# Left factors on VectorE, decoded weights stored and read back, the split of g on VectorE

## The chip, the cores and the metric

One NeuronCore of a Trainium2 chip. The metric is device time in microseconds of one execution of the whole program, as a median over runs. TensorE (PE in the profile), VectorE (DVE), ScalarE (ACT), GpSimd (POOL) and SyncE (SP) each run their own instructions in order; DMA transfers are issued from the queues of SyncE and ScalarE.

## What is computed

Three stages, all in float32, over 4 batches of 768 tokens (3072 rows):

```python
state = gamma * state + outer(k[t], v[t])      # 8 heads of 64, per head
x[t]  = scale * q[t] @ state                   # -> x, 3072 x 512
h = x @ w_in                                   # 512 -> 2048
y = (h - tanh(h)) @ w_out                      # 2048 -> 512
h2 = y @ w_in2                                 # 512 -> 1024
s = h2 * softmax(h2)
out = ((s - mean(s)) / std(s) * g_ln) @ w_out2 # 1024 -> 512
```

The two 2048-wide products are the first layer, the two 1024-wide ones the second. The weights arrive as 64-bit words; the kernel makes float32 of them itself ("decoding").

## The kernel before

Every float32 operand of a matmul is split into a high part and a low rest (both in the matmul's type), and a product is three matmuls: high by high, high by low, low by high. A split is a cast on ScalarE and a subtraction on another engine (`parts`, lines 158 to 160; for weights `stage3`, 147 to 154). A weight block (128 x 512) is decoded by `stage1` (ScalarE) and `stage2` (four operations of VectorE, lines 136 to 144); class `Decoder` steps through load, stage 1, stage 2, stage 3 for a list of blocks.

The tokens fall into six column blocks of 512 (s = 0 to 5). Blocks 0 and 1 take the plain way: attention and `products_h` (line 342) for all 16 blocks f of w_in, then the loop at line 638, which decodes w_out, splits g (`split_g`: `gh` on ScalarE, `gl` on VectorE) and runs `products_y` (line 369) for both; the results go through `ysb` to `y1d` in DRAM (`keep_y`, ScalarE's queue).

Blocks 2 to 5 take h in pairs by a scheme with seven products for a 2 by 2 block product in place of eight. The left factors are sums of four quarters of w_in. `combine_w` (line 499) makes them for one of 8 pairs j: it loads the decoded blocks j and j + 8 from DRAM (`wfd` to `wq`), forms four sums (`wsum`) on GpSimd, splits everything into `wch` (ScalarE) and `wcl` (GpSimd) and stores the four results to `wcd` in DRAM on SyncE's queue; `load_wl` (line 529) reads them back as `wc`. The blocks of w_in get into `wfd` by line 179, from SyncE's queue. The eight combines run at lines 624 and 649, in the last steps of w_in and during the w_out loop.

The loop at line 730 runs 16 steps (two passes, `q`: block pairs 1 and 2, eight j each). One step is 42 matmuls (`product`), interleaved with the next step's first product, and in pass 1 with attention units (`visit`). A product lands in a PSUM bank; `keep` copies it to `part` on ScalarE before the next product adds to the same bank; `summed` adds on VectorE (`hs`), `finish` (line 703) takes the tanh on ScalarE and subtracts on GpSimd or VectorE, and stores g to `gd` on SyncE's queue. From step 13 on the loop also begins to decode w_out again (`dec1`, line 737).

Then the loop at line 800, 64 steps (s, f), 12 matmuls each: `load_g` reads g from `gd`, `split_p` splits it (`gp`, subtraction on VectorE and GpSimd in turn), `dec1.step()` goes on with decoding w_out, `products_y` adds to four banks. In its later part the second layer's weights are decoded and combined (`com`, `dec2`). Last comes the second layer.

Working tiles come from two pools: `t4`, 40 buffers of 4 KB per partition (raw words, `w`, `wc`, `x`), and `t2`, 15 buffers of 2 KB (`wf`, `gh`, `gl`, `g`, `part`, `hs`, `th`). The order on each engine is set by a scheduler that places the instructions by an estimate of time, except where `pin` keeps program order (the first blocks) and for TensorE's order in the passes, the loop at line 800 and the second layer, which is as written.

```python
    def parts(h, o, src, eng):
        nc.scalar.copy(h, src)
        eng.tensor_tensor(o, src, h.bitcast(F32), ALU.subtract)
```

Of the kernel before, what the change touches and what calls it, by code (L numbers as in the profile page):

```python
# [36 lines left out]
P = 128  # L37
# [53 lines left out]
def body(ctx: ExitStack, tc, z, w_in, w_out, w_in2, w_out2, g_ln, cst, tab, out):  # L91
# [23 lines left out]
    wfd = [yd.tile([P, 2, 512], F32, name=f"wfd{j}") for j in range(NJ1)]  # L115
    wcd = [[yd.tile([P, 4, 256], F32, name=f"wcd{j}_{i}") for i in range(4)] for j in range(NJ1)]
# [45 lines left out]
    class Decoder:  # L162
# [6 lines left out]
        def to(self, st, upto, fixed=False):  # L169
            while self.at[st] < min(upto, self.n):  # L170
# [5 lines left out]
                elif st == 2:  # L176
                    stage2(self.raw.pop(i), self.wf[i], fixed)
                    if self.kept and i < NF1:
                        nc.sync.dma_start(out=wfd[i % NJ1][:, i // NJ1, :], in_=self.wf[i])
                else:  # L180
                    self.w[i] = stage3(self.wf.pop(i), self.scales[i], self.eng, fixed)
# [307 lines left out]
    made = [0]  # L489
# [9 lines left out]
    def combine_w():  # L499

        j = made[0]
        made[0] += 1
# [8 lines left out]
        nc.gpsimd.tensor_tensor(t[:, 0, :], a21, a22, ALU.add)  # L511
        nc.gpsimd.tensor_tensor(t[:, 1, :], t[:, 0, :], a11, ALU.subtract)
        nc.gpsimd.tensor_tensor(t[:, 2, :], a11, a21, ALU.subtract)
        nc.gpsimd.tensor_tensor(t[:, 3, :], a12, t[:, 1, :], ALU.subtract)
        for to, lo, n, src in (
# [6 lines left out]
            parts(h, o, src, nc.gpsimd)  # L522
        for i, u in enumerate(ya + yb):
            n = 3 if i < 2 else 4
            nc.sync.dma_start(out=wcd[j][i][:, :n, :], in_=u[:, :n, :].bitcast(F32))
        if j == 0:
            wl[0] = views(ya, yb)
# [80 lines left out]
    for n in range(NF1):  # L608
# [14 lines left out]
        if n in (NF1 - 4, NF1 - 2, NF1 - 1):  # L623
            combine_w()
# [13 lines left out]
    for n in range(NF1 + 1):  # L638
# [9 lines left out]
        if n in (1, 4, 7, 10, 13):  # L648
            combine_w()
        if n == 6:  # L650
            sums[1] = x_sums(1, nc.gpsimd)
# [51 lines left out]
    def finish(s, f, h, eng):  # L703
# [5 lines left out]
        nc.sync.dma_start(out=gd[s][:, f, :], in_=g)  # L709
# [5 lines left out]

    q = [(p, j) for p in (1, 2) for j in range(NJ1)]
    b1, b2, u2, p1, p5 = {}, {}, {}, {}, {}
    dec1 = Decoder([w_out[f] for f in range(NF1)], [None] * NF1, nc.vector)
# [11 lines left out]
    for n in range(len(q) + 1):  # L730
# [3 lines left out]
        if n + 1 < len(q):  # L734
            load_wl(n + 1)
        if now and p == 2 and j >= 5:
            dec1.step()
# [43 lines left out]
    gs, gp = {}, {}  # L781
    steps = [(s, f) for s in range(2, NSB) for f in range(NF1)]

    def load_g(upto):
        while len(gs) < min(upto, len(steps)):
            s, f = steps[len(gs)]
            t = t2([P, SB], F32, "g")
# [228 lines left out]
```

## Time and profile before

| | us |
|---|---|
| median of 3 runs (949.32 to 949.96) | 949.33 |
| the profiled execution, its time | 949.31 |
| its span, first to last instruction | 947.3 |
| TensorE busy in the span | 861.0 (91%) |
| VectorE, ScalarE, GpSimd busy | 572.0, 438.7, 411.7 |
| moved by DMA | 164.54 MB |

The span lies 2.0 us inside the execution's time. A busy time counts an engine's instructions in the trace; an idle time has a releaser, the last event that the waiting instruction needed. In names, `out<-in` are the tiles written and read; L is a line of the kernel.

### The profile page before, as it was taken

To read this page: it belongs to the slowest core of one execution; us is meant where nothing else is said; L and a number is where in the kernel's file an instruction comes from. 1 tells how busy PE (TensorE), PEld (TensorE's weight loads), DVE (VectorE), ACT (ScalarE), POOL (GpSimd) and SP (SyncE) were. 2 spreads that over 40 slices of the span, in tenths; PEclk is the share of its full clock that TensorE was granted. 3 is DMA by queue.
4 is the path that set the end of the run, shared out by engine and by line. 5 is a ranking of instruction groups with operands and counts; after the bars stand their busy time and mean duration, and the time that the engine had idled before them with its cause. 6 is when DMAs were issued, how large, how long until landed. Compare 5 with 4: busy or idle time off the path is not lost.

```text
span 947.3 us, 16798 instructions
## 1 busy us (share of the span) xinstructions
PE 861.0 (91%) x6488; PEld 704.8 (74%) x6488; DVE 572.0 (60%) x993; ACT 438.7 (46%) x850; POOL 411.7 (43%) x340
## 2 busy tenths in 40 slices
PE   5699898697896999999786999999799999999997
PEld 4678687575685777888575888888578888888886
DVE  4688676579872447526688598178455555545542
ACT  4546445354532335545454344144455555444543
POOL 4412116676552456533456285126554444444300
PEclk9799899798998999999997999999999999999999
DMA  9467545765579936994595536182211111111001
GB/s 366 152 224 256 187 162 206 266 206 181 186 258 377 402 142 228 386 389 165 195 388 190 171 112 202 65 284 83 67 44 45 45 45 46 45 45 45 22 23 45
DMA packets 70495, 164.54 MB, mean 174 GB/s; under 512 B 7056, under 2 KB 19472, under 8 KB 70416
## 3 DMA queue, kind: packets, MB, share of 16 engines
q1 hardware_dynamic: 54000, 150.56, 43.9%
q10 hardware_dynamic: 16416, 12.91, 4.2%
q8 instruction: 51, 0.84, 0.3%
q14 instruction: 28, 0.23, 0.1%
HBM read 115.21 MB, written 48.23 MB: 173 GB/s over the span
## 4 chain that ended last, share of the span: by engine, by line
PE 63%; DMA 12%; POOL 7%; DVE 7%; issue 5%; ACT 4%; SPq 1%; ACTq 0%; POOLq 0%; DVEq 0%
PE py L375 16%; PE po L905 14%; PE ph L690 13%; PE ph L841 12%; PE ph L350 3%; DMA wq<-wfd 3%; DMA z<-z 3%; DMA raw<-w_in 2%; PE out L226 2%; PE ptr L891 2%; POOL wcl L160 2%; POOL gp L160 2%; PE sc L226 2%; DMA g<-gd 1%; DVE w L153 1%
## 5 line engine op out<-in xcount | busy, mean ns | idle before, releaser
L375 PE MATMUL py<-gp,w 128*128 128x512 f32 x768 | 179.1, 396 | 15.1 <-POOL gp L160 11.0
L375 PEld LDWEIGHTS py<-gp,w 128*128 128x128 f32 x768 | 147.1, 192 | 47.1 <-POOL gp L160 11.4
L690 PE MATMUL ph<-xh,wc 128*128 128x512 f32 x420 | 134.4, 394 | 2.9 <-ACT part L700 2.1
L905 PE MATMUL po<-w,uh 128*128 128x512 f32 x384 | 118.3, 389 | 0.0
L708 POOL TENSOR_TENSOR hs<-hs,th 128x512 f32<-128x512 f32 x48 | 66.0, 1379 | 104.8 <-ACT th L706 102.8
L375 PE MATMUL py<-gh,w 128*128 128x512 f32 x256 | 85.7, 415 | 17.4 <-ACT gh L363 14.2
L160 POOL TENSOR_TENSOR gp<-g,gp 128x512 fp32r<-128x512 f32 x32 | 66.0, 2069 | 79.7 <-ACT gp L159 79.7
L690 PEld LDWEIGHTS ph<-xh,wc 128*128 128x128 f32 x420 | 78.9, 188 | 21.4 <-ACT part L700 3.3
L350 PE MATMUL ph<-xh,w 128*128 128x512 f32 x256 | 84.3, 404 | 0.0
L905 PEld LDWEIGHTS po<-w,uh 128*128 128x128 f32 x384 | 72.0, 188 | 14.8
L690 PE MATMUL ph<-xl,wc 128*128 128x512 f32 x210 | 81.9, 390 | 0.0
L153 DVE TENSOR_TENSOR w<-wf,w 128x512 fp32r<-128x512 f32 x70 | 66.4, 955 | 22.6 <-ACT w L152 22.3
L905 PE MATMUL po<-w,ul 128*128 128x512 f32 x192 | 74.7, 389 | 0.0
L375 PEld LDWEIGHTS py<-gh,w 128*128 128x128 f32 x256 | 51.1, 201 | 30.4 <-ACT gh L363 15.9
L129 ACT ACTIVATE wf<-raw 128x512 f32<-128x512 f32 x64 | 42.1, 669 | 60.6 <-DMA raw<-w_in 30.1
L482 POOL TENSOR_TENSOR yla<-yl,yha 128x512 fp32r<-128x512 f32 (+1 forms) x24 | 34.1, 1439 | 78.6 <-ACT yha L481 71.3
L152 ACT CAST w<-wf 128x512 fp32r<-128x512 f32 x70 | 42.8, 618 | 55.1 <-DVE wf L143 54.9
L841 PE MATMUL ph<-w,yhs 128*128 128x512 f32 x192 | 63.8, 414 | 3.8 <-ACT part L848 3.7
L713 DVE TENSOR_TENSOR hs<-ph,part 128x512 f32<-128x512 f32 x48 | 33.0, 689 | 48.7 <-PE ph L690 25.0
L375 PE MATMUL py<-gl,w 128*128 128x512 f32 x128 | 52.7, 411 | 7.7 <-DVE gl L366 7.7
L706 ACT ACTIVATE th<-hs 128x512 f32<-128x512 f32 x48 | 30.3, 631 | 63.2 <-DVE hs L713 63.2
L350 PEld LDWEIGHTS ph<-xh,w 128*128 128x128 f32 x256 | 49.6, 194 | 11.2 <-issue 0.2
(126 smaller groups left out, 1740.1 us busy)
## 6 DMA issues: line engine op xcount, KB each, us to landing
z<-z SPq DMA_DIRECT2D x48, 512.0 KB, 7.1
raw<-w_out SPq DMA_DIRECT2D x40, 512.0 KB, 5.8
g<-gd SPq DMA_DIRECT2D x64, 256.0 KB, 4.3
wc<-wcd SPq DMA_DIRECT2D x30, 512.0 KB, 6.9
raw<-w_in SPq DMA_DIRECT2D x24, 512.0 KB, 5.7
gd<-hs SPq DMA_DIRECT2D x48, 256.0 KB, 4.8
wc<-wcd SPq DMA_DIRECT2D x30, 384.0 KB, 6.2
y1d<-ysb ACTq DMA_DIRECT2D x24, 256.0 KB, 4.2
```

Of the source, the lines that this page charges most:

```text
L129: pin(nc.scalar.activation(wf, raw[:, :, 1].bitcast(F32), AF.Abs), fixed)
L152: pin(nc.scalar.copy(hi, wf), fixed)
L153: pin(eng.tensor_tensor(lo, wf, hi.bitcast(F32), ALU.subtract), fixed)
L160: eng.tensor_tensor(o, src, h.bitcast(F32), ALU.subtract)
L226: pin(nc.tensor.matmul(o, a, b, start=True, stop=True, skip_group_check=True), held[0])
L350: nc.tensor.matmul(ph, a[:, k, :], x, start=n == 0, stop=n == 3 * NK - 1), s < 2
L375: nc.tensor.matmul(py[e], a[:, cols], x, start=f == 0 and n == 0, stop=f == NF1 - 1 and n == 2)
L482: nc.gpsimd.tensor_tensor(o, src, h.bitcast(F32), ALU.subtract)
L690: nc.tensor.matmul(ph, a, x, start=first and n == 0, stop=n == 5, skip_group_check=True)
L708: eng.tensor_tensor(g, h, th, ALU.subtract)
L841: nc.tensor.matmul(ph, x[:, r, :], w, start=first and n == 0, stop=n == 5, skip_group_check=True)
L905: nc.tensor.matmul(po, a[:, f, :], b, start=f == 0 and n == 0, stop=f == NF2 - 1 and n == 2)
```

## The change

1. `combine_w` does its sums and its low parts on VectorE and no longer stores; the results stay in SBUF and are used from there in pass 1 (`wl[j]`). `store_w` stores them to `wcd` from ScalarE's queue, for pass 2. Two combines are written into the last steps of w_in, none into the w_out loop, six into the first six steps of pass 1. `load_wl` is called from step 7 on alone.
2. The decoded blocks are stored from ScalarE's queue after the split, those of w_out too (`wod`). The second decoding of w_out goes; `load_wo` reads `wod` and `split_wo` splits it.
3. `finish` puts its g on a list, and ScalarE's queue stores the one of two results before.
4. All splits of g in the last loop of the first layer are on VectorE; the first loads and splits stand before the passes end, and the look-ahead is two steps for splits, five for loads.

```diff
@@ -113,6 +113,7 @@
     mhalf = con[:, C_HALF : C_HALF + 1]
     mask = con[:, C_MASK : C_MASK + D]
     wfd = [yd.tile([P, 2, 512], F32, name=f"wfd{j}") for j in range(NJ1)]
+    wod = [yd.tile([P, 512], F32, name=f"wod{f}") for f in range(NF1)]
     wcd = [[yd.tile([P, 4, 256], F32, name=f"wcd{j}_{i}") for i in range(4)] for j in range(NJ1)]
     gd = {s: yd.tile([P, NF1, SB], F32, name=f"gd{s}") for s in range(2, NSB)}
     y1d = [yd.tile([P, B, NK, P], F32, name=f"y1d{s}") for s in range(NSB)]
@@ -175,10 +176,12 @@
                     self.wf[i] = stage1(self.raw[i], fixed)
                 elif st == 2:
                     stage2(self.raw.pop(i), self.wf[i], fixed)
-                    if self.kept and i < NF1:
-                        nc.sync.dma_start(out=wfd[i % NJ1][:, i // NJ1, :], in_=self.wf[i])
                 else:
-                    self.w[i] = stage3(self.wf.pop(i), self.scales[i], self.eng, fixed)
+                    wf = self.wf.pop(i)
+                    self.w[i] = stage3(wf, self.scales[i], self.eng, fixed)
+                    if self.kept:
+                        to = wfd[i % NJ1][:, i // NJ1, :] if i < NF1 else wod[i - NF1]
+                        pin(nc.scalar.dma_start(out=to, in_=wf), fixed)
                 self.at[st] += 1
 
         def step(self):
@@ -486,7 +489,8 @@
 
 
     wl, xs, sums = {}, {}, {}
-    made = [0]
+    made = []
+    wn = [0]
 
     def views(ya, yb):
         at = {P1: (ya, 0), P2: (ya, 1), P4: (ya, 2)}
@@ -498,8 +502,8 @@
 
     def combine_w():
 
-        j = made[0]
-        made[0] += 1
+        j = wn[0]
+        wn[0] += 1
         w = t4([P, 2, 512], F32, "wq")
         nc.sync.dma_start(out=w, in_=wfd[j])
         a11, a12, a21, a22 = (
@@ -508,10 +512,10 @@
         t = t4([P, 4, 256], F32, "wsum")
         ya, yb = ([t4([P, 4, 256], F32R, "wc" + n) for n in "hl"] for _ in range(2))
         flat = "p a c -> p (a c)"
-        nc.gpsimd.tensor_tensor(t[:, 0, :], a21, a22, ALU.add)
-        nc.gpsimd.tensor_tensor(t[:, 1, :], t[:, 0, :], a11, ALU.subtract)
-        nc.gpsimd.tensor_tensor(t[:, 2, :], a11, a21, ALU.subtract)
-        nc.gpsimd.tensor_tensor(t[:, 3, :], a12, t[:, 1, :], ALU.subtract)
+        nc.vector.tensor_tensor(t[:, 0, :], a21, a22, ALU.add)
+        nc.vector.tensor_tensor(t[:, 1, :], t[:, 0, :], a11, ALU.subtract)
+        nc.vector.tensor_tensor(t[:, 2, :], a11, a21, ALU.subtract)
+        nc.vector.tensor_tensor(t[:, 3, :], a12, t[:, 1, :], ALU.subtract)
         for to, lo, n, src in (
             (ya, 0, 2, w[:, 0, :]),
             (ya, 2, 1, a22),
@@ -519,12 +523,16 @@
             (yb, 2, 2, t[:, 2:4, :].rearrange(flat)),
         ):
             h, o = (u[:, lo : lo + n, :].rearrange(flat) for u in to)
-            parts(h, o, src, nc.gpsimd)
-        for i, u in enumerate(ya + yb):
-            n = 3 if i < 2 else 4
-            nc.sync.dma_start(out=wcd[j][i][:, :n, :], in_=u[:, :n, :].bitcast(F32))
-        if j == 0:
-            wl[0] = views(ya, yb)
+            parts(h, o, src, nc.vector)
+        wl[j] = views(ya, yb)
+        made.append((j, ya + yb))
+
+    def store_w():
+        while made:
+            j, parts_ = made.pop()
+            for i, u in enumerate(parts_):
+                n = 3 if i < 2 else 4
+                nc.scalar.dma_start(out=wcd[j][i][:, :n, :], in_=u[:, :n, :].bitcast(F32))
 
     def load_wl(n):
         t = [t4([P, 4, 256], F32R, "wc") for _ in range(4)]
@@ -620,7 +628,9 @@
         if 2 * B <= k + 1 < 4 * B:
             load_units(min(k + 3, 4 * B))
             prepare(k + 1, H)
-        if n in (NF1 - 4, NF1 - 2, NF1 - 1):
+        if n == NF1 - 1:
+            store_w()
+        if n in (NF1 - 4, NF1 - 1):
             combine_w()
         if n < NF1 - 4:
             dec1.step()
@@ -645,9 +655,9 @@
         if n:
             for b, g in enumerate(gs.pop(n - 1)):
                 products_y(n - 1, g, dec1.w[NF1 + n - 1], py2[b])
-        if n in (1, 4, 7, 10, 13):
-            combine_w()
-        if n == 6:
+        if n == 3:
+            store_w()
+        if n == 4:
             sums[1] = x_sums(1, nc.gpsimd)
         if 8 <= n < 15:
             put_x(1, n - 8, nc.vector)
@@ -706,16 +716,44 @@
         nc.scalar.activation(th, h, AF.Tanh)
         g = th if eng is nc.vector else h
         eng.tensor_tensor(g, h, th, ALU.subtract)
-        nc.sync.dma_start(out=gd[s][:, f, :], in_=g)
+        out_g.append((s, f, g))
+        while len(out_g) > 2:
+            s, f, g = out_g.pop(0)
+            nc.scalar.dma_start(out=gd[s][:, f, :], in_=g)
 
     def summed(ph, part):
         h = t2([P, SB], F32, "hs")
         nc.vector.tensor_tensor(h, ph, part, ALU.add)
         return h
 
+    out_g = []
     q = [(p, j) for p in (1, 2) for j in range(NJ1)]
     b1, b2, u2, p1, p5 = {}, {}, {}, {}, {}
-    dec1 = Decoder([w_out[f] for f in range(NF1)], [None] * NF1, nc.vector)
+    gs, gp = {}, {}
+    steps = [(s, f) for s in range(2, NSB) for f in range(NF1)]
+
+    def load_g(upto):
+        while len(gs) < min(upto, len(steps)):
+            s, f = steps[len(gs)]
+            t = t2([P, SB], F32, "g")
+            nc.sync.dma_start(out=t, in_=gd[s][:, f, :])
+            gs[s, f] = t
+
+    def split_p(n):
+        w = t4([P, 2, SB], F32R, "gp")
+        parts(w[:, 0, :], w[:, 1, :], gs[steps[n]], nc.vector)
+        gp[n] = (w[:, 0, :], w[:, 1, :])
+
+    wo, wof = {}, {}
+
+    def load_wo(upto):
+        while len(wof) < min(upto, NF1):
+            f = len(wof)
+            wof[f] = t2([P, 512], F32, "wf")
+            nc.sync.dma_start(out=wof[f], in_=wod[f])
+
+    def split_wo(f):
+        wo[f] = stage3(wof[f], None, nc.vector, False)
 
     def begin(n):
         b1[n] = bank()
@@ -731,10 +769,18 @@
         now, was = n < len(q), n > 0
         p, j = q[n] if now else (NSB, 0)
         todo = list(per[j]) if p == 1 else []
-        if n + 1 < len(q):
+        store_w()
+        if n + 2 < NJ1:
+            combine_w()
+        elif n + 1 >= NJ1 and n + 1 < len(q):
             load_wl(n + 1)
-        if now and p == 2 and j >= 5:
-            dec1.step()
+        if n == len(q) - 1:
+            load_g(4)
+            load_wo(3)
+        if n == len(q):
+            for i in range(2):
+                split_p(i)
+                split_wo(i)
         if now:
             b3 = bank()
             product(wl[n], P2, b3)
@@ -778,33 +824,19 @@
 
     Y = ExitStack()
     ps_y = Y.enter_context(tc.tile_pool(name="ps_y", bufs=8, space=PSUM, reuse_waits="tile"))
-    gs, gp = {}, {}
-    steps = [(s, f) for s in range(2, NSB) for f in range(NF1)]
-
-    def load_g(upto):
-        while len(gs) < min(upto, len(steps)):
-            s, f = steps[len(gs)]
-            t = t2([P, SB], F32, "g")
-            nc.sync.dma_start(out=t, in_=gd[s][:, f, :])
-            gs[s, f] = t
-
-    def split_p(n):
-        w = t4([P, 2, SB], F32R, "gp")
-        parts(w[:, 0, :], w[:, 1, :], gs[steps[n]], nc.gpsimd if n % 2 else nc.vector)
-        gp[n] = (w[:, 0, :], w[:, 1, :])
-
     nc.sync.dma_start(out=gl, in_=g_ln)
-    load_g(5)
-    for n in range(3):
-        split_p(n)
+    for s, f, g in out_g:
+        nc.scalar.dma_start(out=gd[s][:, f, :], in_=g)
     for n, (s, f) in enumerate(steps):
         if f == 0:
             py = [ps_y.tile([P, SB], F32, tag="y", name="py") for e in range(NK)]
-        if n + 3 < len(steps):
-            load_g(n + 6)
-            split_p(n + 3)
-        dec1.step()
-        products_y(f, gp.pop(n), dec1.w[f], py)
+        load_g(n + 5)
+        load_wo(n + 4)
+        if n + 2 < len(steps):
+            split_p(n + 2)
+        if n + 2 < NF1:
+            split_wo(n + 2)
+        products_y(f, gp.pop(n), wo[f], py)
         if f == NF1 - 1:
             keep_y(s, py)
         if s >= NSB - 3 and n % 2 == 0 and com.n[2] < 12:
```

Three places in the engines' orders. SyncE's queue while w_out is loaded for blocks 0 and 1 (`raw` are loads of encoded weights, `wq` decoded pairs, `wcd` stores of factors). Before:

```order
L525 DMA wcd_0_83<-wch 128x768
L504 DMA wq<-wfd_73 128x1024
L525 DMA wcd_1_84<-wcl 128x768
L525 DMA wcd_2_85<-wch 128x1024
L525 DMA wcd_3_86<-wcl 128x1024
L525 DMA wcd_0_87<-wch 128x768
L525 DMA wcd_1_88<-wcl 128x768
L123 DMA raw<-w_out 128x1024 x3
L525 DMA wcd_2_89<-wch 128x1024
L525 DMA wcd_3_90<-wcl 128x1024
L123 DMA raw<-w_out 128x1024
L504 DMA wq<-wfd_74 128x1024
```

Now:

```order
L508 DMA wq<-wfd_71 128x1024
L124 DMA raw<-w_out 128x1024 x2
L508 DMA wq<-wfd_72 128x1024
L124 DMA raw<-w_out 128x1024 x14
L212 DMA z<-z 128x1024 x4
L508 DMA wq<-wfd_73 128x1024
L212 DMA z<-z 128x1024 x4
L508 DMA wq<-wfd_74 128x1024
L212 DMA z<-z 128x1024 x2
```

The stores are gone from between the loads, which follow each other.

ScalarE at the start of pass 1 (`part` is the copy of a bank, `th` the tanh, `xf` the attention's result). Before:

```order
L700 COPY part<-ph 128x512
L706 ACTIVATE th<-hs 128x512
L700 COPY part<-ph 128x512 x2
L292 COPY xf<-out 128x2x128 x2
L700 COPY part<-ph 128x512
L706 ACTIVATE th<-hs 128x512 x2
L700 COPY part<-ph 128x512
L292 COPY xf<-out 128x2x128 x2
```

Now, around its first combine there:

```order
L160 CAST wch<-wq 128x512
L160 CAST wch<-wq 128x256
L535 DMA wcd_0_111<-wch 128x768
L722 DMA gd_128<-hs 128x512
L160 CAST wch<-wsum 128x512 x2
L535 DMA wcd_1_112<-wcl 128x768
L716 ACTIVATE th<-hs 128x512
L710 COPY part<-ph 128x512
L535 DMA wcd_2_113<-wch 128x1024
L722 DMA gd_127<-hs 128x512
L295 COPY xf<-out 128x2x128 x2
L716 ACTIVATE th<-ph 128x512
```

Casts of a combine and stores of `wcd` and `gd` came between the copies.

VectorE at the start of the loop over `gp` (`w` is the low part of a w_out block). Before, in the middle of the second decoding:

```order
L160 TENSOR_TENSOR gp<-g,gp 128x512
L143 SCALAR_TENSOR_TENSOR wf<-raw,wf 128x512
L140 SCALAR_TENSOR_TENSOR wf<-raw,wf 128x512
L136 TENSOR_SCALAR wf<-wf 128x512
L160 TENSOR_TENSOR gp<-g,gp 128x512
L143 SCALAR_TENSOR_TENSOR wf<-raw,wf 128x512
L137 TENSOR_SCALAR wf<-wf 128x512
L160 TENSOR_TENSOR gp<-g,gp 128x512
L140 SCALAR_TENSOR_TENSOR wf<-raw,wf 128x512
L153 TENSOR_TENSOR w<-wf,w 128x512
L143 SCALAR_TENSOR_TENSOR wf<-raw,wf 128x512
L153 TENSOR_TENSOR w<-wf,w 128x512
```

Now:

```order
L154 TENSOR_TENSOR w<-wf,w 128x512
L161 TENSOR_TENSOR gp<-g,gp 128x512
L154 TENSOR_TENSOR w<-wf,w 128x512
L161 TENSOR_TENSOR gp<-g,gp 128x512
L154 TENSOR_TENSOR w<-wf,w 128x512
L161 TENSOR_TENSOR gp<-g,gp 128x512
L154 TENSOR_TENSOR w<-wf,w 128x512
L161 TENSOR_TENSOR gp<-g,gp 128x512
```

The decode's operations (`wf<-`) are gone; low parts of w_out and of g alternate.

## Rows read from the trace of the kernel before

**Rows 1.** The page: busy us of the engines; TensorE's tenths in 40 slices.

```profile
PE 861.0 (91%) x6488; PEld 704.8 (74%) x6488; DVE 572.0 (60%) x993; ACT 438.7 (46%) x850; POOL 411.7 (43%) x340
...
PE   5699898697896999999786999999799999999997
```

**Rows 2.** TensorE's waits: line and releaser: us in total, times, longest us.

```profile
PE py L375 <- ACT gh L363: 14.2, 4, 8.6
PE py L375 <- POOL gp L160: 11.0, 1, 11.0
...
PE ph L690 <- ACT part L700: 8.1, 3, 6.0
PE py L375 <- DVE gl L366: 7.7, 3, 6.5
```

**Rows 3.** Busy us (instructions) by stretch: PE, PEld, DVE, ACT, POOL; PEclk, DMA, GB/s.

```profile
110.00:150.00 40.00, 36.59 (x467) 29.89 (x459) 25.09 (x52) 18.75 (x48) 8.02 (x9) 0.91 0.44 155
163.80:285.10 121.30, 99.26 (x396) 78.92 (x396) 92.17 (x115) 53.18 (x93) 75.89 (x55) 0.90 0.63 222
...
296.00:367.00 71.00, 71.00 (x1179) 56.39 (x1179) 31.64 (x65) 26.71 (x53) 37.02 (x30) 0.97 0.69 260
...
469.70:515.00 45.30, 30.26 (x113) 24.15 (x114) 37.06 (x63) 22.92 (x40) 26.86 (x8) 0.81 0.78 292
515.00:663.70 148.70, 148.70 (x658) 123.17 (x657) 100.93 (x119) 59.05 (x105) 67.68 (x42) 1.00 0.47 157
```

**Rows 4.** The chain that ended last: start us, us, what.

```profile
295.15 2.93 PE ph L690 x6
...
471.54 5.37 DMA g<-gd
...
488.91 17.14 POOL gp L160
...
699.06 8.16 PE po L905 x36
```

**Rows 5.** Waits from 146 to 296 us on VectorE, ScalarE and SyncE.

```profile
DVE w L153 <- ACT w L152: 15.3, 6, 7.6
...
DVE xl L160 <- ACT xh L159: 7.7, 2, 4.2
...
ACT wch L159 <- POOL wsum L512: 30.3, 7, 6.0
...
SPq L525 <- ACT wch L159: 65.2, 15, 13.4
SPq L525 <- POOL wcl L160: 46.3, 16, 6.3
```

**Rows 6.** Timeline of VectorE and ScalarE, 482 to 488 us: start us, us, operation.

```profile
482.15 0.43 DVE L137 TENSOR_SCALAR wf<-wf 128x512 int32<-128x512 int32 x1
...
485.77 0.69 DVE L153 TENSOR_TENSOR w<-wf,w 128x512 fp32r<-128x512 f32 x1
486.37 0.69 DVE L160 TENSOR_TENSOR gp<-g,gp 128x512 fp32r<-128x512 f32 x1
...
487.69 0.62 ACT L152 CAST w<-wf 128x512 fp32r<-128x512 f32 x1 [0.92 <-DVE wf L143]
```

**Rows 7.** VectorE's groups, 146 to 296 us: busy us, mean ns of one, idle before.

```profile
L366 DVE TENSOR_TENSOR gl<-g,gh 128x512 fp32r<-128x512 f32 x32 | 27.0, 862 | 0.0
```

**Rows 8.** VectorE's groups, 296 to 440 us.

```profile
L331 DVE TENSOR_TENSOR sa<-sb,sc 128x256 f32<-128x256 f32 x4 | 1.6, 411 | 0.0
...
L545 DVE TENSOR_TENSOR xt<-xf 128x1024 f32<-128x1024 f32 x1 | 1.2, 1226 | 0.0
```

**Rows 9.** SyncE's queue: one issue, and its waits from 367 to 440 us.

```profile
469.72 0.32 SPq L709 DMA_DIRECT2D gd<-th  x1
...
SPq L709 <- DMA wc<-wcd: 5.7, 8, 1.2
```

**Rows 10.** Waits from 285 to 296 us.

```profile
ACT part L700 <- DMA y1d<-ysb: 7.7, 1, 7.7
```

## The prediction

> **What bounds the kernel now.** I read first the page's engine totals and slices [rows 1]: TensorE is busy 861.0 of 947.3 us, no other engine above 60%, and before the second layer its digits fall to 6 or 7 in slices 8, 10, 13, 20 and 22 (23.7 us each). So TensorE is the bound, and a change wins only where TensorE idles or runs slowly. The list of its waits [rows 2] says behind whom: ScalarE's `gh` (14.2 us), GpSimd's `gp` (11.0), ScalarE's `part` (8.1), VectorE's `gl` (7.7). The busy times by stretches [rows 3] say where. I call 163.8 to 285.1 us the **py2 stage** (second product of the first two column blocks), 285.1 to 469.7 the **two passes** of seven products, 469.7 to 663.7 the **y stage**. After it comes the second layer, which the change doesn't edit.
>
> Full speed is seen in the second layer: 36 matmuls in 8.16 us [rows 4], 0.2267 us each. The py2 stage has 384 of them, 87.1 us, and 12 small rests, so 88; it takes 121.3. TensorE is busy 99.3 us of that [rows 3]: 22 us are idle, 11 are matmuls at the low clock. The granted clock is 0.90 there, and after a wait at 295.15 us six matmuls take 2.93 us instead of 1.36, which is the lower of the two levels, 1.2 and 2.4 GHz [rows 3, 4]. The y stage has 768 matmuls, 174.1 us, and takes 194.0: in its first 45.3 us TensorE is busy 30.3 at a clock of 0.81 [rows 3], so 15 us are idle and 5 go to the low clock; after that it is dense.
>
> Why TensorE waits in py2: ScalarE runs in order, and its casts of the combined factors (`wch`) waited 30.3 us for GpSimd's `wsum` [rows 5]; the casts `gh` that TensorE needs stood behind them. SyncE's queue waited 65.2 and 46.3 us at L525, the stores of those factors, with loads of w_out behind. And VectorE is slow beside GpSimd: `gl` takes 862 ns on average [rows 7], like operations elsewhere 0.69 us [rows 6].
>
> Why it waits in the y stage: a `gp` on GpSimd took 17.14 us [rows 4], and TensorE stood 11.0 us for it [rows 2], while VectorE was busy 37.1 of 45.3 us [rows 3], mostly decoding w_out a second time.
>
> **The change, part by part.** I sum against the profiled execution's own 949.31 us (span 947.3 and 2.0 around it); the median of the runs is 949.33, so nothing needs shifting.
>
> *Combining on VectorE (py2).* In its new order VectorE has between its first `gl` and its first `hs` 92 operations of 512 columns, 29 tensor_scalar, 9 of 1024 columns and 15 of 256. At 0.69, 0.43, 1.23 and 0.41 us [rows 6, 8] that is 63.5 + 12.5 + 11.1 + 6.2 = 93 us; but operations start 0.60 us apart while each lasts 0.69 [rows 6], so 145 times 0.09, 13 us, may come off. VectorE needs 80 to 93, TensorE 88: near balance. I take 95 for the stage, which is 88 and 7 of hand-overs between ScalarE and VectorE; I put it by the 80-to-93 bound because GpSimd is nearly idle there afterwards. Gain 121.3 - 95 = **26.3**. Ends: 88 (gain 33) and 116 (rival A, gain 5).
>
> The first combine costs VectorE 4.1 us (4 at 0.41, 3 at 0.69, 1 at 0.41) near 110 to 150 us, where it is busy 25.1 of 40 [rows 3]: nothing, under that cover; without it, 4. The 16 stores of `wfd` cost ScalarE's queue 0.32 us each, as an issue did on SyncE [rows 9]; ScalarE is busy 18.8 of those 40 us: nothing; without that room, 5.
>
> *The start of the passes.* TensorE waits 6.0 us there [rows 2], since `part` stood 7.7 us behind `y1d` stores [rows 10]. In the new order eight `y1d` and four `wcd` stores stand there, and SyncE no longer loads `wc`. I take no change; ends a gain of 6 and a loss of 6.
>
> *Inside the passes.* Four combines fall in pass 1: 16 us of VectorE, and on ScalarE four casts each, at most 0.62 [rows 6], plus some 40 issues at 0.32: 10 + 13 us. From 296 to 367 us VectorE is busy 31.6 of 71 and ScalarE 26.7 [rows 3], so both fit, and each factor is made more than one step (42 matmuls, 9.5 us) ahead. What TensorE can feel is ScalarE held by a store: between P6 and P7 of one bank stand P3 and P1, 12 matmuls or 2.7 us, in which `part` must be copied; behind it the tanh that frees banks is queued too. In pass 2 SyncE's stores lost 5.7 us over 8 waits for earlier loads, at most 1.2 each [rows 9], so most would hide; and each `gd` store now comes two results later, so it finds GpSimd done. I take a **loss of 3**, ends 0 and 15.
>
> A rule speaks against these four combines. The row: a GpSimd subtraction took 17.14 us beside a VectorE that hardly paused [rows 4, 3]. The Trainium skill, SBUF — State Buffer, section "Who interferes with whom", says that a VectorE instruction with two SBUF inputs and a GpSimd instruction that reads SBUF exclude each other, each for the whole instruction. By that rule GpSimd would lose only the combines' own time in pass 1, which its idle time there covers, and the sum stays; by the row it can lose far more, which is rival C.
>
> *Pass 2.* The decode of w_out inside it goes, and all its stores leave SyncE. Of `part`'s 8.1 us of waits, 2.1 are not the one at the start [rows 2]; I credit them: **gain 2**, ends 0 and 4.
>
> *The y stage.* The second decode goes (16 times 2 at 0.69 and 2 at 0.43, 36 us of VectorE, and 8 MB of loads); 4 MB of decoded rows are read instead, and all 64 `gp` come to VectorE. Per step TensorE needs 12 matmuls, 2.72 us, VectorE 1.4 (one `gp`, one `w`), ScalarE two casts, 1.2. The first two splits are made before pass 2 ends. Both stalls end and with them the low clock: of 19.9 us I keep 2.2, **gain 17.7**, ends 0 (rival B) and 19.9. Next to be late would be the load of `g`, 5.37 us on the chain [rows 4], but it is issued three to five steps ahead. From 515 us on TensorE is dense and VectorE busy 100.9 of 148.7 [rows 3]; it gets some 32 `gp` more, 22 us, and loses GpSimd's `gp` beside it: nothing; without that room, 5.
>
> The stores themselves get no term. SyncE's waits at L525 [rows 5] are waits for data, and what stands behind them moves up; that is inside the 26.3. The Trainium skill, DMA: Bandwidth & Descriptors, section "Issuing engines are not separate DMA queues", says that issuing from another engine saves only time of issue; by that rule alone they bring nothing either, and A gets likelier.
>
> Sum: 26.3 - 3 + 2 + 17.7 = 43.0; 949.3 - 43.0 = 906.3, so **906 us**.
>
> **Rivals.** *A: py2 stays bound by VectorE and ScalarE waiting for each other.* VectorE waited 15.3 us for `w` casts and 7.7 for `xh` casts [rows 5], and every combine adds such turns. 93 + 15.3 + 7.7 = 116, a gain of 5.3 in place of 26.3: 927 us. Against it: those casts stood behind `wch` casts that waited for GpSimd. *B: the y stage starts no better,* since `g` and `w` come by loads that follow ScalarE's stores: 949.3 - 25.3 = 924. For it: the 5.37 us of that load [rows 4]; against: four `g` and three `w` are loaded one step earlier. *C: ScalarE's queue becomes the bound of pass 1, slower than now.* If GpSimd's `hs` is starved and the stores of `gd` or `wcd` hold `part` beyond the 2.7 us, each of its 8 steps pays as the one at 295.15 did, 6.0 idle and 1.6 at the low clock [rows 2, 4], 61 us: 949.3 - 46 + 61 = 964. It decides from the point where a store waits over 2.7 us in most steps; the 1.2 us [rows 9] speak against it. *D: the change doesn't do what it says,* since the waits only move to the casts of a VectorE that is then as late as GpSimd was: 949.
>
> **How the numbers follow.** Forecast 0.68, A 0.13, B 0.07, C 0.08, D 0.04. The good ends give 33 - 0 + 4 + 20 = 57, so the range starts at 892; it passes A and B and ends at 930, where 3 us of a dearer pass 1 have room. C, D and a tail stay out. A measurement tells 0.2%, 1.9 us, from no change. Faster 0.88, same 0.04, slower 0.08.
>
> **What would show it.** Right: `gh` and `gl` nearly gone from TensorE's waits, py2 near 95 us at a clock near 1, `gl` near 0.69 us, the y stage near 176 us. Wrong: waits of `ph` for `part` of several us in every step of pass 1 (C), VectorE waiting for casts in py2 (A), a first `gp` that waits for its load (B).

## The result and the profile after

The change takes the kernel from 949.33 us (945.72 to 949.96, 4 runs) to 905.11 us (903.46 to 905.39, 4 runs): a ratio of 0.9538, 95% interval 0.9512 to 0.9564. The forecast was 906 in a range of 892 to 930. The profiled execution took 905.02 us, with a span of 903.2; its page answers to [rows 1]:

```profile
PE 852.2 (94%) x6488; PEld 700.9 (78%) x6488; DVE 540.6 (60%) x1025; ACT 430.7 (48%) x834; POOL 281.9 (31%) x244
...
PE   5699999899978899999899999999899999999997
```

TensorE's deep dips of slices 8, 10 and 22 (6 or 7) are gone, and slice 20 has 8 for 7. But slices 12 to 14, the start and the first half of pass 1, show 7, 8 and 8: the dip that stood in slice 13 (6) is flatter and longer. The list of TensorE's waits answers to [rows 2]:

```profile
PE sc L229 <- POOL vq L241: 8.0, 3, 6.5
PE ph L700 <- ACT part L710: 7.2, 4, 3.6
PE sc L229 <- issue: 6.1, 4, 3.5
PE py L378 <- ACT gh L366: 4.7, 1, 4.7
PE ph L700 <- DVE hs L726: 4.4, 2, 2.9
...
PE sc L229 <- POOL vs L252: 3.6, 1, 3.6
```

Of 14.2 us behind `gh` 4.7 are left, nothing behind `gl` and `gp`. `part` is waited for nearly as long as before (8.1). And `sc`, the attention units, now waits inside pass 1 too: 3.7 us of the line with "issue" (no releaser in the profile) and the 3.6 us behind `vs` fall there, where before the change TensorE had no wait after the restart; the rest of the `sc` waits lie in the w_in steps, before and after. So the forecast time came with something lost that was not forecast. The timeline of TensorE gives the sum by stages. The marks are the starts of its first `py` matmul, of pass 1's first product, of the product after the wait for `part` (the restart), of the last attention unit's last products and of the y stage (before: the end of the passes, 469.7), the second layer's first product, and the end of the span:

| stage, us | before | after | gain | forecast |
|---|---|---|---|---|
| w_in steps, to the first `py` | 163.8 | 151.5 | 12.3 | 0 |
| w_out loop (py2), to the first product of pass 1 | 118.3 | 94.8 | 23.6 | 26.3 |
| start of the passes, to the restart | 13.0 | 8.9 | 4.0 | 0 |
| to the last attention unit | 66.3 | 79.6 | -13.4 | -3 |
| to the y stage | 108.3 | 116.9 | -8.6 | +2 |
| y stage | 194.0 | 174.1 | 19.9 | 17.7 |
| second layer | 283.7 | 277.5 | 6.2 | 0 |

Before rounding the gains sum to 44.1, the difference of the spans. Two stages gained about as forecast, the passes lost 22 us where 1 was forecast, and 22.5 us came in three places that were forecast at nothing. The passes by stretches, columns as in [rows 3]; first before, between the same marks:

```profile
295.15:361.41 66.26, 66.26 (x1126) 52.47 (x1130) 28.31 (x61) 24.84 (x49) 33.88 (x29) 0.96 0.73 275
361.41:469.70 108.29, 105.35 (x501) 85.71 (x492) 62.65 (x78) 54.44 (x93) 51.31 (x35) 1.00 0.75 283
```

After:

```profile
255.19:334.82 79.63, 70.78 (x1126) 55.47 (x1130) 46.76 (x93) 32.02 (x65) 35.73 (x29) 0.94 0.70 256
334.82:451.69 116.87, 108.79 (x502) 88.19 (x493) 53.19 (x62) 54.46 (x92) 50.36 (x35) 0.97 0.65 235
451.85:500.00 48.15, 48.15 (x215) 39.85 (x214) 23.04 (x38) 21.26 (x38) 1.29 (x1) 1.00 0.71 235
```

Before the change TensorE was dense up to the last unit; now it idles 8.9 us, and its busy time is 4.5 us longer for as many matmuls, at a clock of 0.94: after the pause shown below, eight matmuls start 0.43 us apart in place of 0.23, the lower of the clock's two levels. VectorE has 18.5 us more work there but is far from full. So VectorE's load alone does not explain the loss; the order does part of it. VectorE's timeline shows the order, and TensorE's beside it (in brackets the idle time before an instruction and what ended it):

```profile
277.95 0.69 DVE L726 TENSOR_TENSOR hs<-ph,part 128x512 f32<-128x512 f32 x1 [1.57 <-PE ph L700]
284.27 0.43 DVE L515 TENSOR_TENSOR wsum<-wq 128x256 f32<-128x256 f32 x1 [5.63 <-DMA wq<-wfd]
284.61 0.42 DVE L517 TENSOR_TENSOR wsum<-wq 128x256 f32<-128x256 f32 x1
284.94 0.75 DVE L303 TENSOR_TENSOR xf<-xf,out 128x256 f32<-128x256 f32 x2
```

```profile
281.56 0.39 PE L700 MATMUL ph<-xh,wcl 128*128 128x512 f32 x1
285.46 1.00 PE L229 MATMUL sc<-qs,z 64*64 64x64 f32 x30 [3.51 <-issue]
```

VectorE stood 5.63 us for the load of `wq`, with two attention adds (`xf`) behind it. The profile names no releaser for TensorE's 3.51 us, but its unit went on while these adds ran; the run with earlier loads tests the link. Only four of the six combines written into pass 1 run there: the scheduler put two at the end of the w_out loop.

### The profile page after: what moved, and what is told of

It is laid out like the page before. It is cut to its first block, busy times and chain, and to the rows that moved or that the text cites. A ratio compares the mean times of both kernels' runs of the same rounds, so it can differ in the third digit from the quotient of the medians.

```text
span 903.2 us, 16591 instructions
## 1 busy us (share of the span) xinstructions
PE 852.2 (94%) x6488; PEld 700.9 (78%) x6488; DVE 540.6 (60%) x1025; ACT 430.7 (48%) x834; POOL 281.9 (31%) x244
## 4 chain that ended last, share of the span: by engine, by line
PE 80%; DMA 6%; issue 5%; DVE 3%; POOL 3%; ACT 2%; ACTq 0%; SPq 0%; POOLq 0%; DVEq 0%
PE py L378 28%; PE po L937 14%; PE ph L873 12%; PE ph L700 10%; PE ph L353 9%; DMA wc<-wcd 2%; PE ptr L923 2%; PE out L229 2%; POOL hs L718 2%; PE sc L229 1%; DMA z<-z 1%; DMA raw<-w_in 1%; DMA y1d<-ysb 1%; POOL qs L241 1%; DVE wcl L161 1%
## 5 line engine op out<-in xcount | busy, mean ns | idle before, releaser
L378 PE MATMUL py<-gp,w 128*128 128x512 f32 x768 | 174.2, 389 | 0.0
L378 PEld LDWEIGHTS py<-gp,w 128*128 128x128 f32 x768 | 144.1, 188 | 29.9
L378 PE MATMUL py<-gh,w 128*128 128x512 f32 x256 | 81.6, 399 | 4.7 <-ACT gh L366 4.7
L700 PE MATMUL ph<-xh,wc 128*128 128x512 f32 x224 | 72.8, 402 | 6.2 <-ACT part L710 3.3
L937 PE MATMUL po<-w,ul 128*128 128x512 f32 x192 | 74.8, 389 | 0.0
L154 DVE TENSOR_TENSOR w<-wf,w 128x512 fp32r<-128x512 f32 x70 | 52.9, 759 | 13.1 <-ACT w L153 12.4
L161 DVE TENSOR_TENSOR gp<-g,gp 128x512 fp32r<-128x512 f32 x64 | 46.1, 740 | 19.8 <-ACT gp L160 19.8
L700 PEld LDWEIGHTS ph<-xh,wc 128*128 128x128 f32 x224 | 43.7, 195 | 16.8 <-ACT part L710 4.1
L700 PE MATMUL ph<-xh,wch 128*128 128x512 f32 x112 | 47.2, 422 | 5.5 <-ACT part L710 4.0
L898 ACT ACTIVATE ex<-hn,nm 128x1024 f32<-128x1024 f32 x24 | 27.7, 1153 | 50.9 <-DVE nm L888 50.3
L378 PE MATMUL py<-gl,w 128*128 128x512 f32 x128 | 50.5, 395 | 0.0
```

The lines of the kernel that those rows point to most:

```text
L154: pin(eng.tensor_tensor(lo, wf, hi.bitcast(F32), ALU.subtract), fixed)
L378: nc.tensor.matmul(py[e], a[:, cols], x, start=f == 0 and n == 0, stop=f == NF1 - 1 and n == 2)
L700: nc.tensor.matmul(ph, a, x, start=first and n == 0, stop=n == 5, skip_group_check=True)
L937: nc.tensor.matmul(po, a[:, f, :], b, start=f == 0 and n == 0, stop=f == NF2 - 1 and n == 2)
```

## The experiments

Ratios are to runs of the kernel before on the same chip; "scaled" is the ratio times 949.33 us, where the change has 905.5. Stages are taken between the marks above, from one profiled execution of each kernel; where no wait for `part` marks the restart, two stages stand as one. The names of the rows stand in the headings below.

| kernel | w_in | w_out | start | to last unit | to y | y stage | 2nd layer | ratio (95%) | scaled |
|---|---|---|---|---|---|---|---|---|---|
| the change | 151.5 | 94.8 | 8.9 | 79.6 | 116.9 | 174.1 | 277.5 | 0.9538 (0.9512 to 0.9564) | 905.5 |
| e1_wfd_sync | 166.3 | 94.7 | 9.3 | 82.9 | 117.0 | 174.1 | 277.7 | 0.9633 (0.9584 to 0.9682) | 914.5 |
| e2_all_early | 151.6 | 106.6 | 8.9 | 67.0 | 116.0 | 174.2 | 277.7 | 0.9499 (0.9474 to 0.9525) | 901.8 |
| e3_wq_ahead | 150.3 | 94.1 | 6.3 | 75.9 | 115.2 | 174.1 | 277.0 | 0.9428 (0.9400 to 0.9457) | 895.0 |
| e4_gd_sync | 150.8 | 94.1 | 7.9 | 79.6 | 110.3 | 174.2 | 277.5 | 0.9436 (0.9402 to 0.9470) | 895.8 |
| e5_gp_half | 151.4 | 94.2 | 9.3 | 78.8 | 117.4 | 174.2 | 281.8 | 0.9591 (0.9561 to 0.9621) | 910.5 |
| e6_decode_again | 151.2 | 94.5 | 7.9 | 80.6 | 120.4 | 174.2 | 277.9 | 0.9550 (0.9514 to 0.9587) | 906.6 |
| e9_gp_half_decode | 152.2 | 94.2 | 7.9 | 83.3 | 120.5 | 188.2 | 281.5 | 0.9735 (0.9691 to 0.9778) | 924.2 |
| e10_early_pool | 153.4 | 120.3 | 8.3 | 68.8 | 114.3 | 174.2 | 277.7 | 0.9653 (0.9621 to 0.9686) | 916.4 |
| e7_comb_pool | 152.3 | 94.7 | 8.3 | 78.6 | 118.2 | 174.1 | 276.8 | 0.9495 (0.9432 to 0.9558) | 901.4 |
| f1_both | 151.1 | 94.7 | 7.2 | 75.6 | 110.6 | 174.2 | 276.8 | 0.9378 (0.9354 to 0.9402) | 890.3 |
| f3_y_sync | 149.6 | 94.8 | 80.9 | (in it) | 110.4 | 174.2 | 276.6 | 0.9350 (0.9328 to 0.9373) | 887.6 |
| f4_three_early | 150.2 | 94.3 | 74.8 | (in it) | 110.0 | 174.2 | 277.3 | 0.9299 (0.9269 to 0.9328) | 882.8 |

All edits are to the changed kernel.

**Stores of w_in on SyncE again (e1_wfd_sync).**

```diff
                     stage2(self.raw.pop(i), self.wf[i], fixed)
+                    if self.kept and i < NF1:
+                        nc.sync.dma_start(out=wfd[i % NJ1][:, i // NJ1, :], in_=self.wf[i])
...
-                    if self.kept:
-                        to = wfd[i % NJ1][:, i // NJ1, :] if i < NF1 else wod[i - NF1]
-                        pin(nc.scalar.dma_start(out=to, in_=wf), fixed)
+                    if self.kept and i >= NF1:
+                        pin(nc.scalar.dma_start(out=wod[i - NF1], in_=wf), fixed)
```

> Only the stores of the 16 decoded w_in blocks go back to SyncE's queue, right after their decoding. Theory Q: in the kernel before they made a loop (a load of raw weights could be issued only after the store of the block before, and that only after its decoding), and this loop is why the last h product ended at 160.7 us there and at 151.5 us now. Then the w_in steps take 7 to 10 us longer again and the whole 912 to 915 us, with ScalarE waiting over 5 us at a time for raw loads. Rival: the stores cost their issue alone, and the 9 us came from the combines that left these steps: 905 us, within 2.

Measured: 918.97 us (911.89 to 923.73), scaled 9 us above the change; the w_in steps are 14.8 us longer in the profiled execution, which was the longest of the four; besides, the stretch to the last unit is 3.3 us longer. That is theory Q, with the steps dearer than its 7 to 10 us. The run's SyncE queue shows the loop (timeline; the store `wfd`, and the load of `raw` that could not be issued before it):

```profile
109.88 0.33 SPq L180 DMA_DIRECT2D wfd<-wf  x1
110.30 0.87 SPq L213 DMA_DIRECT2D z<-z  x2
111.27 0.37 SPq L124 DMA_DIRECT2D raw<-w_in  x1
120.77 0.33 SPq L180 DMA_DIRECT2D wfd<-wf  x1
```

and ScalarE's waits from 60 to 166 us show who pays (27.2 us in 8 waits in the kernel before; in the change this line does not occur):

```profile
ACT wf L130 <- DMA raw<-w_in: 31.9, 9, 6.6
```

A load, its decoding, the store that waits for it, the next load: one round every 11 us.

**All combines early, on VectorE (e2_all_early).** In the w_in steps and the w_out loop `combine_w` stands where it stood before; pass 1 loads all factors but the first:

```diff
-        if n + 2 < NJ1:
-            combine_w()
-        elif n + 1 >= NJ1 and n + 1 < len(q):
+        if n + 1 < len(q):
             load_wl(n + 1)
```

> The eight combines stand where they stood before (three in the w_in steps, five in the w_out loop), still on VectorE and stored from ScalarE's queue; pass 1 reads the factors back. Theory V: the passes lost 22 us (196.7 us from the restart of TensorE to the y stage, against 174.6 before) because combines inside pass 1 make VectorE wait for the load of wq and hold what TensorE needs behind it. Then that stretch takes 175 to 180 us. VectorE was full in the first 43 us of the w_out loop and had 13.6 us free in the next 45, so 20 us of combines lengthen that loop by 7 to 20: 892 to 906 us in all. Rival S: it is ScalarE, held by stores of g that wait for loads of wc; then the stretch stays above 190 us and the whole goes to 910 to 920.

Measured: 904.10 us, by the ratios not told apart from the change. From the restart to the last unit 67.0 us, as before the change (66.3): 12.6 of the 13.4 us lost there go when no combine stands inside pass 1. The rest of the passes stays at 116.0, so theory V has one half of the loss and not the other: the two stretches take 183.0 us together, between its 180 and the 190 of rival S. The w_out loop pays 11.8 us; by the trace six combines run there, where in the change three do (one at its start and two at its end).

**Earlier loads of `wq` (e3_wq_ahead).** Each is written a step before its combine, the first of them in step 12 of the w_out loop:

```diff
         if n + 2 < NJ1:
             combine_w()
+            if n + 3 < NJ1:
+                load_wq(n + 3)
```

> The load of wq for each combine in pass 1 is written one step earlier, so that in SyncE's queue it stands ahead of the loads of z. Theory V: VectorE's waits for wq (9.1 us in 3 waits) end and with them TensorE's stalls of 3.51 and 3.57 us and some of the low clock after each: 895 to 899 us. Rival: the loads are late because their buffers come free late, and whichever load stands behind is late instead: 903 to 908 us, with TensorE waiting for attention units.

Measured: 897.71 us. VectorE's waits for `wq` (9.1 us in the change) are gone, the stretch to the last unit is 3.7 us shorter, the start 2.6. Theory V's time, but only part of its place: TensorE now waits 5.2 us in 3 waits for an add of VectorE (`sa`) there. So the load of `wq` accounts for 3.7 of the 13.4 us lost up to the last unit; the other 9 or so go only with the combines themselves, and no run shows what in them costs it.

**Stores of g on SyncE again (e4_gd_sync).**

```diff
-        out_g.append((s, f, g))
-        while len(out_g) > 2:
-            s, f, g = out_g.pop(0)
-            nc.scalar.dma_start(out=gd[s][:, f, :], in_=g)
+        nc.sync.dma_start(out=gd[s][:, f, :], in_=g)
```

> Each g is stored at once from SyncE's queue, as before; the rest of the change stays. Theory S: ScalarE was held 8.5 us in 3 waits by stores of g that wait for loads of wc; without them the stall of 2.93 us at 385 us and its low clock go, 900 to 902 us. Theory V: ScalarE's stores cost little and SyncE's loads now stand behind them again: 905 to 912 us.

Measured: 897.97 us, better than theory S. The stretch to the y stage is 6.6 us shorter. ScalarE's waits from 330 us to the end of the passes; the change:

```profile
ACT th L716 <- DVE hs L726: 30.9, 21, 3.8
ACT th L716 <- DMA wc<-wcd: 8.5, 3, 4.0
```

With the stores on SyncE the second line does not occur:

```profile
ACT th L716 <- DVE hs L723: 39.1, 28, 2.5
ACT part L710 <- PE ph L700: 6.0, 8, 0.8
```

A tanh does not read `wc`; the store of g ahead of it in ScalarE's queue was what waited until a load of `wc` had landed. The longest of the three, on ScalarE:

```profile
371.90 0.59 ACT L710 COPY part<-ph 128x512 f32<-128x512 f32 x1 [0.67 <-POOL hs L718]
376.06 0.33 ACTq L722 DMA_DIRECT2D gd<-th  x1
376.48 0.63 ACT L716 ACTIVATE th<-hs 128x512 f32<-128x512 f32 x1 [4.00 <-DMA wc<-wcd]
```

What ties a store to a load that it shares no data with stands in the trace, which keeps the semaphore that tells of each transfer's landing. The program's 413 transfers share eight of them, over both queues, and in all 405 cases where one follows another on the same semaphore it was issued after the earlier had landed. The store at 376.06 us has the semaphore of a load issued at 367.40 and landed at 375.98; the other two stores that waited share theirs with loads in the same way.

**The y stage: GpSimd, the second decoding, both.** Three kernels: the first edit (e5_gp_half), the second (e6_decode_again, in part here), the two together (e9_gp_half_decode).

```diff
-        parts(w[:, 0, :], w[:, 1, :], gs[steps[n]], nc.vector)
+        parts(w[:, 0, :], w[:, 1, :], gs[steps[n]], nc.gpsimd if n % 2 else nc.vector)
```

```diff
-        load_wo(n + 4)
...
-        if n + 2 < NF1:
-            split_wo(n + 2)
-        products_y(f, gp.pop(n), wo[f], py)
+        dec1.step()
+        products_y(f, gp.pop(n), dec1.w[f], py)
```

> Every second split of g goes back to GpSimd; w_out is still read back and not decoded again. Theory G: the wait in the y stage came from GpSimd itself, whose subtraction took 17.14 us in the kernel before; then the y stage grows from 174.1 to 180 to 190 us, and the second layer, whose first left factors GpSimd makes, loses its 6 us again: 912 to 925 us. Rival H: GpSimd was starved only beside the second decoding that filled VectorE; without it the y stage stays within 2 us of 174 and the whole at 905 to 908.

Measured: 911.73 us; the y stage stays at 174.2, as rival H has it, but the second layer loses 4.3 us, as theory G has it; the whole lies below G's range and above H's.

> w_out is decoded a second time, as before (from step 13 of the passes on), and not stored or read back; all splits of g stay on VectorE. Theory H: the second decoding was the cause, 36 us of VectorE against 45 us of the stage's start; then the y stage takes 182 to 194 us and the whole 913 to 925. Theory G: with GpSimd out of it VectorE keeps up; the y stage stays at 174 to 178 and the whole at 905 to 909.

Measured: 908.06 us, by the ratios not told apart from the change; the y stage stays at 174.2 (theory G), and the end of the passes is 3.5 us longer.

> Both at once: every second split of g on GpSimd and w_out decoded a second time. Each alone left the y stage at 174.2 us. Theory J (either is enough): the two together bring the wait back, a GpSimd split of 8 us or more beside a full VectorE, and the y stage takes 182 to 194 us, the whole 916 to 928. Theory K: the wait went with something else in this part of the change (the first splits before the passes end, the load of g five steps ahead); then the y stage stays at 174 to 177 and the whole is 910 to 914, the sum of the two small losses seen.

Measured: 925.38 us, the y stage 188.2: theory J. TensorE's wait is back, and the list of the instructions on `gp` (count, then ns at the least, in the median, at the most) has the long subtraction:

```profile
PE py L378 <- POOL gp L161: 10.9, 1, 10.9
```

```profile
L161 POOL TENSOR_TENSOR gp<-g,gp x32: 1286/1683/16540, 447.0 to 637.1; 128x512 fp32r<-128x512 f32 x32
```

With GpSimd alone the longest was

```profile
L161 POOL TENSOR_TENSOR gp<-g,gp x32: 1288/1574/3776, 442.6 to 616.0; 128x512 fp32r<-128x512 f32 x32
```

During those 16.54 us VectorE ran 32 instructions and was busy for 16.50 (third of the five engines):

```profile
472.04:488.58 16.54, 5.66 (x25) 4.34 (x24) 16.50 (x32) 8.39 (x15) 16.54 (x2) 0.77 0.53 202
```

So in the y stage either half of the change would have done.

**Combines on GpSimd.** `combine_w` as before the change (`nc.gpsimd` for its eight operations), stored from ScalarE's queue; once with all combines early (e10_early_pool), once at the places of the change (e7_comb_pool).

> As the run with all eight combines at their old places, but their sums and low parts on GpSimd again; the stores of the factors stay on ScalarE's queue. With VectorE that w_out loop took 106.6 us, in the kernel before 118.3. Theory P: GpSimd was the slow part (ScalarE's casts waited 30.3 us for its sums), so the loop goes to 113 to 120 us and the whole to 911 to 918. Theory Q (SyncE's queue was the slow part, with loads of w_out behind stores that waited 65 and 46 us): the loop stays at 103 to 108 and the whole at 900 to 906.

Measured: 916.34 us, the loop 120.3: theory P. With VectorE it was 106.6, so the engine brings 13.7 us. Before the change the loop took 118.3 with the stores on SyncE's queue: the other queue brought nothing that shows, though this run also stores the 16 blocks of w_out there, and the two were not tried apart.

> The places of the combines as in the change (two in the w_in steps, six in pass 1), but sums and low parts on GpSimd. Theory P (GpSimd is too slow for them): by the rows of the run with all eight early on GpSimd one combine is about 11 us there (four sums of 0.9 to 1.5 us, three low parts of 1.7 to 2.1 and one of 0.8); six are 66 us, beside the 44 us that GpSimd already had between the restart and the last attention unit, a stretch of 80 us. Then this stretch takes 100 to 115 us and the whole 922 to 940. Theory V (VectorE is the wrong place inside pass 1, since TensorE waits behind its waits for wq): the stretch stays below 82 us and the whole at 903 to 908.

Measured: 904.31 us (899.54 to 909.00), the stretch 78.6. Theory P is wrong: inside pass 1 the engine makes no difference that the runs tell. V's numbers came, but not its reason, since on GpSimd the stretch is as long. GpSimd's groups for the low parts, in the w_out loop with all combines early:

```profile
L161 POOL TENSOR_TENSOR wcl<-wsum,wch 128x512 fp32r<-128x512 f32 x14 | 23.8, 1716 | 1.2 <-ACT wch L160 1.2
L161 POOL TENSOR_TENSOR wcl<-wq,wch 128x512 fp32r<-128x512 f32 x7 | 14.7, 2101 | 26.8 <-ACT wch L160 26.8
```

and at the places of the change, 250 to 345 us:

```profile
L161 POOL TENSOR_TENSOR wcl<-wsum,wch 128x512 fp32r<-128x512 f32 x10 | 12.7, 1287 | 2.5 <-ACT wch L160 2.5
L161 POOL TENSOR_TENSOR wcl<-wq,wch 128x512 fp32r<-128x512 f32 x4 | 5.2, 1295 | 0.0
```

The same operation takes 1.29 us here, where VectorE is busy 28.0 of 78.6 us, and 1.72 to 2.10 there, where it is busy 92.9 of 120.4. My estimate took the dear price, and six combines instead of the four that run there.

**Put together.** Both edits that won (f1_both); then y1d on SyncE's queue as well (f3_y_sync); then three combines written into the second half of the w_out loop, their factors read back in pass 1 (f4_three_early):

```diff
-            nc.scalar.dma_start(
+            nc.sync.dma_start(
                 out=y1d[s][:, :, e, :], in_=ysb.rearrange("p (j t) -> p j t", j=B)
...
+        if n in (9, 11, 13):
+            store_w()
+            combine_w()
```

> The two edits that each won alone, together: wq loaded a step ahead in pass 1, and each g stored at once from SyncE's queue. If they take away different waits (wq ahead shortened the stretch to the last attention unit by 3.7 us, the stores the one behind it by 6.9) the gains add: 889 to 893 us. If SyncE's stores of g now hold the loads of wq, the first gain is lost: 896 to 899.

Measured: 891.29 us (890.29 to 892.11), in the range of the first case. By stages the gains add: 4.0 us up to the last unit and 6.3 behind it, where each edit alone had 3.7 and 6.6 (the text above has 6.9). By the scaled times 15.2 us are gained, and 10.5 and 9.7 by each alone; with each of the four ratios uncertain by 2 to 3 us, the runs cannot tell whether the missing 5 us are real.

> As the run with both edits, and the y1d stores of the first two blocks and of the later ones leave ScalarE's queue for SyncE's. TensorE stood 3.6 us at the start of pass 1 for a copy that was queued behind these stores, with matmuls at the lower clock behind it. If ScalarE's queue is what holds that copy, the start (8.9 us from the first product to the restart) falls to about 5 and the whole is 2 to 4 us below the run with both edits. If the copy waits for the same transfers through a buffer, or SyncE's loads now stand behind the stores: no gain or a loss of up to 4.

Measured: 888.55 us (888.33 to 888.90), 2.7 us better on the same chip. TensorE's wait for `part` at the start of pass 1 (3.6 us in the change, 1.6 in the run with both edits) does not occur: the copy stood behind ScalarE's stores of y1d.

> As the run with y1d stored from SyncE's queue, but three of the six combines of pass 1 stand in the second half of the w_out loop, where VectorE had 13.6 us free of 45.3; they need 12.3 (4.1 each), and their factors are stored and read back. With all eight early the stretch from the first product of pass 1 to the last attention unit took 75.9 us, here 80.9 with six in pass 1: with three, 78. If the free time holds them, the whole falls by about 3 us to 884 to 887; if the w_out loop grows by more than 3 us (TensorE waits for gh behind their casts), it is 888 to 893.

Measured: 883.14 us (882.27 to 884.02); scaled, 23 us better than the change. The w_out loop now holds three combines in its second half (two in the change) and stays at 94.3 us, so the free time held them. Pass 1 holds three where it held four, not six as the text above counts; and from pass 1's first product to the last unit it takes 74.8 us (before 79.2, the change 88.6). Its page:

```profile
PE 840.9 (95%) x6488; PEld 693.6 (79%) x6488; DVE 544.5 (62%) x1025; ACT 431.1 (49%) x834; POOL 280.4 (32%) x244
...
PE   4799999799999899999899999999899999999997
```

## Why the prediction was right, and where not

The two large terms were right, in cause and nearly in size: 43.5 of the 66 us gained. But the losses in the passes were forecast 21 us too small, and 22.5 us of gains were missing from the sum. The two errors cancel, so that the time came out within 1 us is luck.

- **py2.** The stage was forecast at 95 and took 94.8 us; TensorE has one wait there, 4.7 us for `gh`. VectorE is as near the balance as forecast, 82.3 of 94.8 us busy, and 43.2 of 43.3 us between 161.7 and 205 us; its `gl` takes 718 ns on average, before 862 [rows 7]. The gain is 23.6 and not 26.3, because the 121.3 us that I set against it hold pass 1's first 12 matmuls. What gains is shown: the combines' engine 13.7 us in this loop, taking three of them out of it 11.8 more. Rivals A and D fell.
- **"The stores themselves get no term"** failed for the stores of w_in. I had looked at SyncE's waits at L525 only. In the w_in steps each store stood ahead of the load that ScalarE waited for next; putting them back costs 9 us by the ratios and 14.8 in the profile. The first combine and the `wfd` issues cost nothing, as forecast: TensorE is dense from 110 to 150 us. The rule of the Trainium skill, DMA: Bandwidth & Descriptors, section "Issuing engines are not separate DMA queues", fits the stores of the factors (120.3 against 118.3 us, with the reserve made above) and not these: what the other queue saved was not time of issue but the wait at the head of the queue.
- **"Inside the passes: loss of 3, ends 0 and 15"** was mis-sized: 13.4 up to the last unit, near the far end. 12.6 of it come with the four combines. I priced their engine time, which fits (16 us of VectorE; 18.5 measured), and what ScalarE's stores could hold; what VectorE's wait for `wq` holds was in no term, and is worth 3.7. The rest stays open: it is neither the engine (78.6 us on GpSimd) nor the wait for `wq`.
- **"In pass 2 ... at most 1.2 each, so most would hide", a gain of 2**: it lost 8.6, outside its ends. That is rival C's mechanism a pass later: the waits that SyncE's stores had for loads of `wc` came to ScalarE with the stores, up to 4.0 us and 8.5 in three waits. Moving them back gives 6.6. The time of C (964) did not come, since three stores waited so and not one in every step.
- **The start** gained 4.0, inside its ends; the range's lower end left its possible gain of 6 out. That `part` stands behind y1d stores is shown; why the start is 4 us shorter wasn't tried.
- **The y stage** kept all of 19.9. Both stalls ended, and the low clock with them (granted clock 1.00 up to 500 us, 0.81 before [rows 3]), as forecast, and rival B fell. But the two edits, each summed as needed, cover for one another.
- **The second layer** got no term, as "the change doesn't edit" it; it gained 6.2. 4.3 of it goes when GpSimd has its splits back. TensorE then waits 2.1 us for `part` at the stage's start, before the change 3.7, in the change not at all, and the granted clock in the first 36 us is 0.91, 0.91 and 0.95. What in GpSimd's work makes that copy late isn't shown, and the rest wasn't tried.
- The rule of the Trainium skill, SBUF — State Buffer, section "Who interferes with whom", agrees with the traces as to who: GpSimd's long subtractions stand beside a full VectorE, its short ones beside one that is a third busy. How long it lasts is more than I read out of it: 16.54 us is a whole train of 32 VectorE instructions. In pass 1 it decided nothing (79.6 us with VectorE, 78.6 with GpSimd).

## What to carry to other kernels

Cost a moved operation by what it waits for and what stands behind it on its new queue, not by its engine time alone: of the terms that failed here, wherever the cause was found it was a queue's head waiting (VectorE for `wq`, ScalarE's store for `wc`, SyncE's store for a decoded block). A store belongs on a queue whose next entries nobody needs soon; where a store of late data stands ahead of the loads that feed the same loop, each round waits for the one before. Where transfers share a few semaphores, an issue can also wait for another queue's transfer, and on a computing engine the computing behind it waits too. And where two edits remove one stall, test them apart: one may be enough, and the other is free to be put where it costs less.

## What was not expected of the hardware

- A GpSimd subtraction of 128x512, 1.29 us where VectorE is a third busy, lasted 16.54 us beside 32 VectorE instructions with 0.04 us of pauses in all.
- A store issued by ScalarE waited up to 4.0 us until loads issued by SyncE had landed, though it shares no data with them, and ScalarE's computing stood still for that time. What ties them is in the program: eight landing semaphores for all transfers of both queues, each used again only after its last transfer has landed (405 of 405 cases).
